# The sine products of a Fourier mixer's hidden layer, from the third chunk on, as three products of 12-bit parts

## The chip, the cores and the metric

The kernel runs on one core of a Trainium2 chip. The metric is the time of one execution on the device in microseconds (us); the kernel before took 1809.15 us (median of three runs, 1809.08 to 1809.34). A core has a matrix engine (TensorE, PE in the rows, its weight loads in rows of their own, PEld), a vector engine (DVE), a scalar engine (ACT), a general one (POOL), and a queue that issues transfers (SP). Each works through its own instructions in order and waits on semaphores for the others.

## The reference

```python
def _attn_ref(x):                       # x: (8, 3008, 256) float32
    X = np.fft.fft(x, axis=1)           # along the sequence
    X = np.fft.fft(X, axis=2)           # along the features
    return X.real.astype(np.float32)

def _moe_ref(x, w_in, w_out):           # x: (24064, 256), w_in: (256, 2048), w_out: (2048, 256)
    h = x @ w_in
    g = np.maximum(0.01 * h, h)         # leaky ReLU
    return (g @ w_out).astype(np.float32)
```

The output is `_moe_ref` of the mixed x, reshaped to 24064 rows. All is float32.

## The kernel before

**Mixing.** The transform along the sequence is done by matrix products with cosine and sine tables after several rounds of folding; the one along the features is folded into `w_in`. Rows k and S-k of the mixed x have the form cos + sin and cos - sin. So the core keeps, for one batch at a time, a cosine half `mix_sb[0]` and a sine half `mix_sb[1]` of 128 partitions by 1505 columns (and the Nyquist row `nb_sb`), and the up product of a pair of rows is one product with the cosine half and one with the sine half. `transform` makes the two halves of one batch and parity, `rows_of_x(0, c)` (cosine) first, then `rows_of_x(1, c)`. Its vector work is put in a list, `folds`, from which `some` emits a little at each step.

**Chunks.** After a first stage of 504 columns with an order written out by hand (`HEAD`, `START`) come 23 chunks of 504 or 498 columns, three to a batch (two in the first). A chunk has 16 steps, one for each 128 rows of the hidden layer (index f). In step f, `up` issues the cosine product into `cos_ps` and the sine product into `sin_ps` (two banks of each, used by turns), each 128 by 128 by 504. ACT copies the cosine bank to `cos_sb` and writes the seed of step f+2 (the Nyquist row times a weight) into the bank; DVE makes cos + sin and cos - sin (`hidden`, the line `nc.vector.tensor_tensor(block.row(to, g, self.n), x, y, op=op)`, L1266); ACT applies the leaky ReLU to them one step later (L1529). The down products use a fast scheme for matrix products: 28 sums of hidden blocks (`SUMS`, on POOL and DVE, L1283), 26 times 4 products of 252 columns (`PRODUCTS`, L1304) with weights that SP streams from memory into a ring `wr`, and 34 sums of results (L1350) on DVE.

**Order.** The program is written out in the order of a list of events, sorted by a time in steps: kind 3 is an up product (at `16 t + 1.20 + f`), kind 1 a sum, kind 2 a down product (6.5 for each step), kind 0 the start of a step, where transforms and loads go on. Each engine's instructions stand in the order in which they are emitted; every engine waits at the front of its own list. A POOL sum is in places made to wait for the DVE instruction ahead of it (`wait_for_gate`).

**Names.** `wf` holds the folded `w_in`, its cosine part (index 0) and its sine part (index 1), in one tile that is const; `block_sb` holds 28 slots of hidden blocks and sums, `part_sb` 24 places for results, `wr` 9 weights.

Of the kernel before, what the change touches and what calls it, by code (L numbers as in the profile page):

```python
# [9 lines left out]
F32 = mybir.dt.float32  # L10
I32 = mybir.dt.int32
# [5 lines left out]
P = 128  # L17
# [310 lines left out]
def tile_fnet_leaky_relu(  # L328
# [21 lines left out]

    block_sb = const.tile([P, SLOTS * SS], F32, name="block")
# [18 lines left out]
    def ring(tag):  # L370
# [5 lines left out]
    assert weights_at - 4 * P >= lay_out(block_sb, 0, (("g", 5, 2 * WN), ("win", 4, WN), ("power", 2, WN), ("raw", 1, 2 * WN), ("o", 2, 2 * WN),  # L376
                                               ("e", 2, 2 * WN), ("s", 4, 2 * WN)))
    head_at = {
        "part": [part_sb, lay_out(part_sb, 0, (("cos", 3, WN), ("out", 2, 2 * WN), ("we", 1, WN), ("nyq", 1, UW[0]))), PARTS * NMAX],
        "cos": [cos_sb.rearrange("p a n -> p (a n)"), 0, 4 * NMAX],  # L380
    }
# [8 lines left out]
    rings["ev"] = [0, [ev_sb, in_head(KC)]]  # L390
    rings["e0"] = [0, [e0_sb, in_head(384)]]
# [100 lines left out]
    class Rows:  # L492
# [3 lines left out]
        def __init__(self, src, scratch, part, c):  # L496
            self.src, self.scratch, self.part, self.c = src[0:ROWS], scratch, part, c
            self.places = PLACES[c] if part else range(16)
# [36 lines left out]
    def rows_of_x(part, c):  # L535

        src = x3[:, 1 - c, :, part * P : (part + 1) * P]
        return Rows(src, [x3[:, 2 * c].rearrange("p c (i d) -> p (c i) d", i=2)], part, c)
# [46 lines left out]
    wf = const.tile([P, 2, F], F32, name="wf")  # L585
# [3 lines left out]
    wt = block_sb[:, weights_at:].rearrange("p (i g n) -> p i g n", g=4, n=P)  # L589
    w_dram = dram.tile([8 + len(W_SUMS), P, 4 * P], F32, name="w_dram")  # L590
    feat_sb = block_sb[:, weights_at - 4 * P : weights_at].rearrange("p (a n) -> p a n", a=2)
    nyx = in_parts(4 * NT * B, 2, 2, NT, B)[0:LOADED]
    nyz = in_parts(16 * B, 16, B)[0:LOADED]
# [120 lines left out]
    def fold_w_in(f0, n, made, tag="up", pieces=1, queue=nc.sync, sums=None):  # L714
# [13 lines left out]
        for odd, at in places:  # L728
            w = m if odd else n
            for i in (1, 0):  # L730
                rows = slice(half, P) if i != odd else slice(0, half)
                nc.scalar.copy(wf[rows, i, f0 + at : f0 + at + w], banks[odd, at][rows, 0:w])
                if i == 1 and odd == 0:
                    spread_wn(f0, n, queue)

    def spread_wn(f0, n, queue):

        for q in range(f0 // P, (f0 + n) // P):
            queue.dma_start(wn[:, q : q + 1], wf[P // 2 : P // 2 + 1, 1, q * P : (q + 1) * P])
# [58 lines left out]

    reach = [w % 4 for w in range(8)]
# [4 lines left out]
    stream = Stream()  # L804
# [219 lines left out]
    def raised(j, f):  # L1024
        b, c, at, n, _ = blocks[j]
        fs = hidden_blocks(j, f)
        pt = raw[j, f] = seeded.get((j, f)) or [up_ps(), up_ps()]
        for blk in range(2):
            for h in range(2):
                nc.tensor.matmul(pt[blk][:, h * n : (h + 1) * n], lhsT=wf[:, blk, fs[h] * P : (fs[h] + 1) * P],  # L1030
                                 rhs=mix_sb[blk][:, at : at + n], start=(h == 0 and (blk == 1 or (j, f) not in seeded)),
                                 stop=(h == 1), skip_group_check=True)
# [186 lines left out]
    class Chunk:  # L1219
# [22 lines left out]
        def touch(self, f, since):  # L1242

            nc.tensor.matmul(cos_ps[self.half(f)][:, since : self.w], lhsT=wf[:, 0, 0:P], rhs=mix_sb[0][:, since : self.w],
                             start=False, stop=True, skip_group_check=True)

# [3 lines left out]
        def up(self, f):  # L1250
            cos, sin = cos_ps[self.half(f)], sin_ps[self.half(f)]
            for i, bank in enumerate((cos, sin)):
                nc.tensor.matmul(bank[:, 0 : self.w], lhsT=wf[:, i, f * P : (f + 1) * P], rhs=mix_sb[i][:, self.lo : self.lo + self.w],  # L1253
                                 start=(i == 1), stop=True, skip_group_check=True)
            k, g = divmod(f, 4)
# [4 lines left out]
            return k, g, copy, sin  # L1260

# [122 lines left out]
    def transform(u, gate):  # L1384
# [4 lines left out]
        first, second = (rows_of_x(part, c) for part in range(2))  # L1389
        for rows in (first, second):  # L1390
            if rows is first:
                load_tabs(0, c)
            rows.fold_even(folds, folds)
            rows.fold_odd(folds, folds)
            if rows is first:
                yield 0, ahead
                made = mix(u, 0, v=folds)
                made[0](even_rows(first, P))
                load_tabs(1, c, (0,))
# [36 lines left out]
    def rest():  # L1436

        count = len(chunk)
        every.extend(Chunk(t) for t in range(count))
        events = []  # L1440
        for t in range(count):
            for f in range(NF):
                events.append((16 * t + UP_FROM + f, 3, t, f))
            for i, s in enumerate(SUMS_AT):
                events.append((16 * t + (s if t < count - 1 else max(s - LAST_SOONER, min(s, 17.05))), 1, t, i))
            for m in range(4 * len(PRODUCTS)):
                events.append((16 * t + (DOWN_FROM + m / PER_STEP if t else FIRST_DOWN + m / FIRST_PER), 2, t, m))
        for r in range(16 * count + 18):
# [50 lines left out]
        for _, kind, t, i in events:  # L1499
            if kind == 0:  # L1500
                start_work(16 * t + i)
                now[0] = START_SHARES.get(i, 0.0) if 16 * t + i < 17 else SHARES[0] if 16 * t + i < 32 else SHARES[1]
# [17 lines left out]
            else:  # L1520
# [11 lines left out]
                behind[:] = [None]  # L1532
                waiting[:] = [part.hidden(*made)]
# [245 lines left out]
```

## Time and profile before

| what | value |
|---|---|
| median of 3 runs | 1809.15 us |
| profiled execution: span from first to last instruction | 1807.9 us |
| median less span (what lies around the span) | 1.25 us |
| PE / DVE / ACT / POOL busy | 100% / 85% / 58% / 57% |
| transfers | 245.88 MB, 136 GB/s over the span |
| granted TensorE clock | 1.000 |

The profile gives no time of the profiled execution other than its span; the median of the runs lies 1.25 us above it. Rows of the timeline read: start in us, length in us, engine, line, operation, what it writes and reads, shape, how many instructions in a row, and in brackets how long the engine had been idle and for whom. A float32 product shows as two MATMUL instructions (x2), each with a weight load. Ends of matmuls are modelled, so the distance from one start to the next, not the length, tells what a product takes.

### The profile page before, as it was taken

Reading aid. Unit: us, or ns where it says so; the run is one execution under the profiler, and the core shown is the slowest. Engines: PE = TensorE matmul, PEld = TensorE weight load, DVE = VectorE, ACT = ScalarE, POOL = GpSimd, SP = SyncE. Lnnn points to the kernel's source line nnn. Section 1 sums busy time; section 2 is a strip of 40 time slices with the busy share of each in tenths; the row PEclk is TensorE's granted clock in tenths of the full one; section 3 lists DMA queues with packets and bytes.
Section 4 is the critical chain, followed back from the end, with each engine's and each line's share of the span. In section 5 each row is a group of like instructions: output and inputs, shape, how many; then the busy total and the mean of one; then the engine's idle time right before and its main releaser. Section 6 shows DMA issues by size and latency. Waiting matters only on the chain.

```text
span 1807.9 us, 22509 instructions
## 1 busy us (share of the span) xinstructions
PE 1801.6 (100%) x7232; PEld 1336.7 (74%) x7232; DVE 1535.2 (85%) x2614; ACT 1042.9 (58%) x1785; POOL 1034.3 (57%) x443
## 2 busy tenths in 40 slices
PE   9999999999999999999999999999999999999999
PEld 7867777777777777777777777777777777777778
DVE  8899888788798987999869988789887897876868
ACT  4687556665556655665556655566555665555540
POOL 2236666766565665755656656556566565566730
PEclk9999999999999999999999999999999999999999
DMA  7365345433363333624435234443333533323324
GB/s 253 104 216 177 95 136 171 149 118 103 117 199 115 122 117 116 223 79 137 135 128 182 90 119 133 150 160 114 128 132 125 173 124 115 122 90 109 121 90 153
DMA packets 144115, 245.88 MB, mean 136 GB/s; under 512 B 17392, under 2 KB 53872, under 8 KB 144000
## 3 DMA queue, kind: packets, MB, share of 16 engines
q1 hardware_dynamic: 143856, 244.46, 41.5%
q8 instruction: 58, 0.95, 0.2%
q14 instruction: 57, 0.47, 0.1%
q10 hardware_dynamic: 144, 0.00, 0.0%
HBM read 212.86 MB, written 31.54 MB: 135 GB/s over the span
## 4 chain that ended last, share of the span: by engine, by line
PE 97%; DVE 1%; ACT 1%; DMA 0%; issue 0%; DVEq 0%
PE sum_psc L1304 21%; PE sum_psa L1304 17%; PE sum_psb L1304 17%; PE sin_psb L1253 9%; PE cos_psb L1253 9%; PE cos_psa L1253 8%; PE sin_psa L1253 8%; PE dft_ps L838 3%; PE sum_psa L1075 1%; PE sum_psc L1075 1%; PE sum_psb L1075 1%; PE dft_ps L1075 1%; PE cos_psa L1030 0%; PE sin_psa L1030 0%; DMA block<-in_w_in_dram 0%; PE sin_psb L1030 0%
## 5 line engine op out<-in xcount | busy, mean ns | idle before, releaser
L1283 POOL TENSOR_TENSOR block<-block 128x1008 f32<-128x1008 f32 (+1 forms) x396 | 995.5, 2525 | 620.2 <-DVE xt L1096 164.1
L1304 PE MATMUL sum_psc<-block,wr 128*128 128x252 f32 (+1 forms) x1832 | 426.0, 375 | 0.8 <-DMA wr<-w_dram 0.8
L1283 DVE TENSOR_TENSOR block<-block 128x1008 f32<-128x1008 f32 (+1 forms) x248 | 417.2, 1687 | 1.5 <-POOL block L1283 1.4
L1304 PEld LDWEIGHTS sum_psc<-block,wr 128*128 128x128 f32 x1832 | 347.8, 190 | 94.7 <-issue 60.4
L1529 ACT ACTIVATE block<-block 128x504 f32<-128x504 f32 (+3 forms) x510 | 393.2, 798 | 4.5 <-DVE block L1266 4.4
L1266 DVE TENSOR_TENSOR block<-cos,sin_psa 128x504 f32<-128x504 f32 (+1 forms) x356 | 224.3, 671 | 150.1 <-PE sin_psa L1253 149.5
L1304 PE MATMUL sum_psb<-block,wr 128*128 128x252 f32 (+1 forms) x1472 | 347.4, 376 | 0.0
L1304 PE MATMUL sum_psa<-block,wr 128*128 128x252 f32 (+1 forms) x1480 | 344.6, 376 | 0.0
L1304 PEld LDWEIGHTS sum_psb<-block,wr 128*128 128x128 f32 x1472 | 277.5, 190 | 85.2 <-issue 56.2
L1304 PEld LDWEIGHTS sum_psa<-block,wr 128*128 128x128 f32 x1480 | 280.5, 190 | 68.2 <-issue 41.0
L1266 DVE TENSOR_TENSOR block<-cos,sin_psb 128x504 f32<-128x504 f32 (+1 forms) x380 | 239.3, 671 | 93.5 <-PE sin_psb L1253 91.9
L1259 ACT COPY cos<-cos_psb 128x504 f32<-128x504 f32 (+1 forms) x190 | 109.5, 576 | 243.5 <-PE cos_psb L1253 243.5
L1259 ACT COPY cos<-cos_psa 128x504 f32<-128x504 f32 (+1 forms) x178 | 102.7, 577 | 244.4 <-PE cos_psa L1253 244.4
L1253 PE MATMUL sin_psb<-mixs,wf 128*128 128x504 f32 (+1 forms) x380 | 191.2, 585 | 0.6 <-DVE block L1266 0.6
L1253 PE MATMUL cos_psb<-mixc,wf 128*128 128x504 f32 (+1 forms) x380 | 191.0, 585 | 0.0
L1350 DVE TENSOR_TENSOR part<-part 128x252 f32<-128x252 f32 (+1 forms) x342 | 183.1, 573 | 1.3
L1253 PE MATMUL cos_psa<-mixc,wf 128*128 128x504 f32 (+1 forms) x356 | 178.9, 584 | 0.0
L1253 PE MATMUL sin_psa<-mixs,wf 128*128 128x504 f32 (+1 forms) x356 | 178.9, 584 | 0.0
L1253 PEld LDWEIGHTS sin_psb<-mixs,wf 128*128 128x128 f32 x380 | 72.1, 190 | 88.9 <-issue 72.9
L1248 ACT ACTIVATE cos_psb<-nb,small 128x504 f32<-128x504 f32 (+1 forms) x190 | 129.8, 683 | 6.2
L1253 PEld LDWEIGHTS sin_psa<-mixs,wf 128*128 128x128 f32 x356 | 67.7, 190 | 82.0 <-issue 67.3
L1248 ACT ACTIVATE cos_psa<-nb,small 128x504 f32<-128x504 f32 (+1 forms) x178 | 121.6, 683 | 5.8
(213 smaller groups left out, 1329.6 us busy)
## 6 DMA issues: line engine op xcount, KB each, us to landing
wr<-w_dram SPq DMA_DIRECT2D x575, 256.0 KB, 3.5
xt<-in_x_dram SPq DMA_DIRECT2D x28, 1024.0 KB, 7.1
out_dram<-part SPq DMA_DIRECT2D x120, 126.0 KB, 1.8
out_dram<-part SPq DMA_DIRECT2D x64, 124.5 KB, 2.0
tabe<-in_seq_tab_dram SPq DMA_DIRECT2D x29, 190.0 KB, 4.0
w_dram<-block SPq DMA_DIRECT2D x18, 256.0 KB, 7.1
block<-in_w_in_dram SPq DMA_DIRECT2D x8, 512.0 KB, 4.4
block<-in_w_out_dram SPq DMA_DIRECT2D x8, 512.0 KB, 5.1
```

The source lines that it names most:

```text
L838: nc.tensor.matmul(o, lhsT=still, rhs=moving, start=(i == 0), stop=(i == 3), skip_group_check=True)
L1075: nc.tensor.matmul(sums[j][d][:, r * n : (r + 1) * n], lhsT=wo[:, fs[h] // 4, fs[h] % 4, d], rhs=a[r][h], start=(f == 0 and r == 0 and h = ...
L1248: nc.scalar.activation(cos_ps[self.half(f)][:, 0 : self.w], nb_sb[:, self.lo : self.lo + self.w], ACT.Copy, scale=wn[:, f : f + 1])
L1253: nc.tensor.matmul(bank[:, 0 : self.w], lhsT=wf[:, i, f * P : (f + 1) * P], rhs=mix_sb[i][:, self.lo : self.lo + self.w], start=(i == 1), ...
L1259: nc.scalar.copy(copy, cos[:, 0 : self.w])
L1266: nc.vector.tensor_tensor(block.row(to, g, self.n), x, y, op=op)
L1283: ins = (engine or nc.gpsimd).tensor_tensor(self.value(16 + i), xa, ya, op=ALU.add if sign > 0 else ALU.subtract)
L1304: nc.tensor.matmul(to, lhsT=stream.weight(self.t, q, g), rhs=self.value(v)[:, g], start=(first and at == 0), stop=(last and g == 3), skip_ ...
L1350: ins = nc.vector.tensor_tensor(part_of[self.copy[v]][:, 0:n], xa, ya, op=ALU.add if sign > 0 else ALU.subtract)
L1529: nc.scalar.activation(to, to, ACT.Lrelu)
```

## The change

From chunk 2 on (21 of the 23 chunks) the sine product of a step is made of three products in the type float32r. Moving and stationary operand are cut into a high part of 12 bits and a low part: high = x times (1 - 2^-13), rounded on writing; for the weights low = (w - high) times 2^12 and both = low - high; for the moving operand low = x - high and both = (1 + 2^-12) high - x. Two products of the parts (index 0 and 1) go into the sine bank, ACT multiplies the bank by 1 + 2^-12 in place, and the third (index 2) is added 0.2 steps later, by an event of a new kind 5, which then issues `hidden` as well. The cosine product is as before.

The parts of the weights are made once, in steps 18 to 25 (during chunk 1), by `parted_weights` on ACT and POOL in turn, stored to memory, and loaded again for each step into four places that the sine part of `wf` leaves free. The parts of the moving operand are made once for each chunk by `parts` on ACT, DVE and POOL, 2.7 steps ahead of the chunk (kind 4). As that reads the sine half before the chunk begins, `transform` now makes the sine half first. To make room, `SLOTS` goes from 28 to 27, `PARTS` from 24 to 18 and `RING` from 9 to 8; some tiles of the first stage move into the new tiles.

```diff
+SLOTS, RS, SS, PARTS = 27, 252, 1008, 18        (was 28, ..., 24)
+RING, RING_AHEAD = 8, 6                         (was 9, 6)
+PARTED_FROM = 2
+UPPER, SHIFT = 1.0 - 2.0**-13, 2.0**12
+PARTS_AT, PARTED_WEIGHTS_AT, UP_END = -2.7, 18, 0.2
...
+    def parted_weights(f):
...
+        nc.scalar.activation(high, src, ACT.Copy, scale=UPPER)
+        wait_for_gate(nc.gpsimd.tensor_tensor(both, src, high, op=ALU.subtract))
+        nc.scalar.activation(low, both, ACT.Copy, scale=SHIFT)
+        nc.gpsimd.tensor_tensor(both, low, high, op=ALU.subtract)
+        nc.sync.dma_start(parted_dram[f : f + 2].rearrange("f p n -> p f n"), here.bitcast(F32).rearrange("p f i n -> p f (i n)"))
...
+    class Parted:
...
+        def load(self, i):
+            n = F // WN
+            if i >= self.count:
+                return
+            if i < n:
+                self.places.append(late.tile([P, 3 * P], F32R, name=f"parted{i}", tag=f"wf{i}"))
+            nc.sync.dma_start(self.places[i % n].bitcast(F32), parted_dram[i % NF])
...
+        def parts(self):
+            m = mixed[self.t % 2].rearrange("p (i n) -> p i n", i=3)
+            high, low, both = (m[:, i, 0 : self.w] for i in range(3))
+            src = mix_sb[1][:, self.lo : self.lo + self.w]
+            nc.scalar.activation(high, src, ACT.Copy, scale=UPPER)
+            nc.vector.scalar_tensor_tensor(both, in0=high, scalar=1.0 + 1.0 / SHIFT, in1=src, op0=ALU.mult, op1=ALU.subtract)
+            nc.gpsimd.tensor_tensor(low, src, high, op=ALU.subtract)
+        def product_of_parts(self, bank, at, i, start=False):
+            m = mixed[self.t % 2].rearrange("p (i n) -> p i n", i=3)
+            nc.tensor.matmul(bank[:, 0 : self.w], lhsT=parted.weight(at, i), rhs=m[:, i, 0 : self.w],
+                             start=start, stop=True, skip_group_check=True)
...
         def up(self, f):
             cos, sin = cos_ps[self.half(f)], sin_ps[self.half(f)]
-            for i, bank in enumerate((cos, sin)):
+            in_parts = self.t >= PARTED_FROM
+            if in_parts:
+                at = NF * (self.t - PARTED_FROM) + f
+                self.product_of_parts(sin, at, 0, start=True)
+                self.product_of_parts(sin, at, 1)
+                nc.scalar.activation(sin[:, 0 : self.w], sin[:, 0 : self.w], ACT.Copy, scale=1.0 + 1.0 / SHIFT)
+            for i, bank in enumerate((cos, sin)[: 2 - in_parts]):
...
+        def up_end(self, f):
+            at = NF * (self.t - PARTED_FROM) + f
+            self.product_of_parts(sin_ps[self.half(f)], at, 2)
+            parted.load(at + F // WN)
...
-        first, second = (rows_of_x(part, c) for part in range(2))
+        first, second = (rows_of_x(1 - i, c, i == 1) for i in range(2))
```

In the two order listings of each place below, `mixed` is the tile of the moving operand's parts, `parted` a place of the weights' parts, and numbers in names tell tiles apart. On PE, in the middle of a chunk, before:

```order
L1253 MATMUL cos_psa<-mixc,wf 128x504
L1253 MATMUL sin_psa<-mixs,wf 128x504
L1304 MATMUL sum_psa<-block,wr 128x252 x6
L1253 MATMUL cos_psb<-mixc,wf 128x504
L1253 MATMUL sin_psb<-mixs,wf 128x504
L1304 MATMUL sum_psb<-block,wr 128x252 x7
```

and in a like step of the changed kernel, on PE (L1315 is the product of parts, L1330 the cosine product, L1388 a down product):

```order
L1315 MATMUL sin_psb<-mixed_966,parted_1155 128x504 x2
L1330 MATMUL cos_psb<-mixc,wf_cos 128x504
L1388 MATMUL sum_psc<-block,wr 128x252
L1315 MATMUL sin_psb<-mixed_966,parted_1155 128x504
L1388 MATMUL sum_psa<-block,wr 128x252 x6
```

The sine products now stand ahead of the cosine product but for the third, which stands behind exactly one down product. On ACT, at step 12 of the chunk that starts at 956 us in the profile, before (copy of the cosine bank, seed, copy of rows of x, leaky ReLU):

```order
L1321 COPY part<-sum_psb 128x252
L1259 COPY cos<-cos_psa 128x504
L1248 ACTIVATE cos_psa<-nb,small 128x504
L1113 COPY dft_ps<-xt 128x512
L1529 ACTIVATE block<-block 128x4x252
L1259 COPY cos<-cos_psb 128x504
```

and now, on ACT at the same place (L1328 scales the bank, L1309 makes the high part of the next chunk's moving operand):

```order
L1405 COPY part<-sum_psb 128x252
L1328 ACTIVATE sin_psa<-sin_psa 128x504
L1338 COPY cos<-cos_psa 128x504
L1319 ACTIVATE cos_psa<-nb,small 128x504
L1168 COPY dft_ps<-xt 128x512
L1622 ACTIVATE block<-block 128x2x252 x2
L1309 ACTIVATE mixed_966<-mixs 128x498
L1328 ACTIVATE sin_psb<-sin_psb 128x504
```

The scaling stands first in the step, the high part last, behind the leaky ReLU. On DVE at the same step, before:

```order
L1094 TENSOR_TENSOR xt<-xt,dft_ps 128x512
L1350 TENSOR_TENSOR part<-part 128x252
L1096 TENSOR_TENSOR xt<-xt 128x512
L1266 TENSOR_TENSOR block<-cos,sin_psa 128x2x252 x2
L1350 TENSOR_TENSOR part<-sum_psb,part 128x252
```

and now, on DVE (L1310 makes the part called both from the high part; L1350 is now `hidden`, L1434 a sum of results):

```order
L1149 TENSOR_TENSOR xt<-xt,dft_ps 128x512
L1434 TENSOR_TENSOR part<-part 128x252
L1151 TENSOR_TENSOR xt<-xt 128x512
L1310 SCALAR_TENSOR_TENSOR mixed_966<-mixed_966,mixs 128x498
L1350 TENSOR_TENSOR block<-cos,sin_psa 128x2x252 x2
L1434 TENSOR_TENSOR part<-sum_psb,part 128x252
```

L1310 stands ahead of that step's `hidden`, and reads what ACT's L1309 writes behind the leaky ReLU of the same step.

More of the change, by code (lines that the diff above doesn't have):

```diff
@@ L10 @@
 F32 = mybir.dt.float32
+F32R = mybir.dt.float32r
 I32 = mybir.dt.int32
@@ L492, in tile_fnet_leaky_relu, with __init__ @@
     class Rows:
-        def __init__(self, src, scratch, part, c):
+        def __init__(self, src, scratch, part, c, second=False):
             self.src, self.scratch, self.part, self.c = src[0:ROWS], scratch, part, c
-            self.places = PLACES[c] if part else range(16)
+            self.places = PLACES[c] if second else range(16)
         def z(self, i, n=None):
@@ L582, in odd_rows_even, with wf @@
             return po
-    wf = const.tile([P, 2, F], F32, name="wf")
+    wf_cos = const.tile([P, F], F32, name="wf_cos")
+    wf_sin = [late.tile([P, WN], F32, name=f"wf_sin{i}", tag=f"wf{i}") for i in range(F // WN)]
+    def wf(i, at, n):
+        if i == 0:
+            return wf_cos[:, at : at + n]
+        return wf_sin[at // WN][:, at % WN : at % WN + n]
     wn = small_sb[:, 0:NF]
@@ L797, in used, with __init__, weight @@
             self.load_to(self.of[t, q] + 1 + RING_AHEAD)
+    mixed = []
+    def parted_weights(f):
+        if not mixed:
+            mixed.extend(late.tile([P, 6 * NMAX], F32R, name=f"mixed{i}", tag=f"mixed{i}") for i in range(2))
+        here = mixed[f // 2 % 2][:, 0 : 6 * P].rearrange("p (f i n) -> p f i n", f=2, i=3)
+        src = wf(1, f * P, 2 * P).rearrange("p (f n) -> p f n", f=2)
+        high, low, both = (here[:, :, i] for i in range(3))
+        nc.scalar.activation(high, src, ACT.Copy, scale=UPPER)
[4 more added lines that the diff above has]
+    class Parted:
+        def __init__(self):
+            self.places, self.count = [], NF * (len(chunk) - PARTED_FROM)
+        def load(self, i):
[5 more added lines that the diff above has]
+            nc.sync.dma_start(self.places[i % n].bitcast(F32), parted_dram[i % NF])
+        def weight(self, i, part):
+            return self.places[i % (F // WN)][:, part * P : (part + 1) * P]
     reach = [w % 4 for w in range(8)]
@@ L803, in tile_fnet_leaky_relu @@
     by_reach = sorted(range(8, len(reach)), key=lambda w: reach[w])
-    stream = Stream()
+    stream, parted = Stream(), None
     def even_rows(rows, m):
@@ L1519, in rest @@
                         some(pool)
-            else:
+            elif kind == 4:
+                every[t].parts()
+            elif kind == 3:
                 if i == 0:
@@ L1532, in rest @@
                 behind[:] = [None]
+                waiting.clear()
+            else:
+                part = every[t]
+                if t >= PARTED_FROM:
+                    part.up_end(i)
                 waiting[:] = [part.hidden(*made)]
```

56 lines of the change are left out of this document (35 added, 21 removed).

## The prediction

> **What bounds the kernel now.** I read the page's busy shares and its chain first, to learn which engine sets the end.
>
> ```profile
> PE 1801.6 (100%) x7232; PEld 1336.7 (74%) x7232; DVE 1535.2 (85%) x2614; ACT 1042.9 (58%) x1785; POOL 1034.3 (57%) x443
> PE 97%; DVE 1%; ACT 1%; DMA 0%; issue 0%; DVEq 0%
> ```
>
> PE is never idle and is 97% of the chain, so every PE microsecond taken away shortens the end, as long as nothing else makes PE wait. What the change takes away I read from the timeline of one step:
>
> ```profile
> 899.83 1.01 PE L1253 MATMUL cos_psa<-mixc,wf 128*128 128x504 f32 x2
> ...
> 900.68 1.01 PE L1253 MATMUL sin_psa<-mixs,wf 128*128 128x504 f32 x2
> 900.68 0.19 PEld L1253 LDWEIGHTS sin_psa<-mixs,wf 128*128 128x128 f32 x1 [0.23 <-issue]
> 900.88 0.58 ACT L1259 COPY cos<-cos_psa 128x504 f32<-128x504 f32 x1 [1.76 <-PE cos_psa L1253]
> ...
> 901.52 2.68 PE L1304 MATMUL sum_psc<-block,wr 128*128 128x249 f32 x12
> 901.52 2.29 PEld L1304 LDWEIGHTS sum_psc<-block,wr 128*128 128x128 f32 x11 [0.23 <-issue]
> ...
> 904.04 1.01 PE L1253 MATMUL cos_psb<-mixc,wf 128*128 128x504 f32 x2
> ```
>
> Start to start a sine product takes 901.52 - 900.68 = 0.84 us (0.845 over several steps), in two instructions of 0.42. The 12 instructions of 249 columns take 904.04 - 901.52 = 2.52, 0.21 each, with 11 weight loads in 2.29 beside them; a load by itself shows 0.19. A step is 2 x 0.845 + 6 (or 7) x 0.42 = 4.22 (or 4.64). ACT sees a product 900.88 - 900.68 = 0.20 after the next one starts.
>
> The next engines are read from the windows of three chunks of one batch (columns: PE, PEld, DVE, ACT, POOL busy) and one of chunk 1:
>
> ```profile
> core 0: us, PE busy (x) PEld busy (x) DVE busy (x) ACT busy (x) POOL busy (x), PEclk, DMA share, GB/s
> 150.00:222.00 72.00, 72.00 (x295) 53.27 (x294) 65.64 (x110) 43.00 (x73) 45.38 (x18) 1.00 0.37 115
> 956.00:1028.00 72.00, 72.00 (x275) 52.12 (x274) 66.21 (x101) 45.89 (x78) 42.84 (x18) 1.00 0.44 140
> 1028.00:1102.00 74.00, 74.00 (x304) 55.14 (x303) 63.90 (x111) 42.94 (x75) 45.75 (x20) 1.00 0.37 119
> 1102.00:1176.00 74.00, 74.00 (x304) 55.14 (x303) 58.85 (x111) 41.86 (x77) 46.21 (x19) 1.00 0.43 142
> ```
>
> DVE has 72 - 66.2 = 5.8 us left in the first chunk of a batch, 10.1 and 15.2 in the others; ACT and POOL have 26 and more. The waits tell who is ahead of whom:
>
> ```profile
> ACT cos L1259 <- PE cos_psa L1253: 244.4, 167, 2.4
> ACT cos L1259 <- PE cos_psb L1253: 243.5, 181, 2.0
> DVE block L1266 <- PE sin_psa L1253: 149.5, 93, 4.0
> DVE block L1266 <- PE sin_psb L1253: 91.9, 64, 3.8
> ```
>
> ACT waits for PE in 348 of 368 steps, 1.4 us each. DVE waits for the sine product in only 157; in the others it comes late, and PE does not mind.
>
> **The PE term.** In 21 chunks x 16 = 336 steps a product of 0.845 gives way to three of float32r, whose price no row shows. Cutting both operands at 12 bits leaves one of the four part-products that a full 24-bit product consists of, so I price one at a quarter of 0.845, 0.211. The upper end is 0.42, one of the two instructions that the float32 product shows; the quarter is the lower end, since one part-product of the four is the least that is left. By the quarter a step gains 0.845 - 0.634 = 0.211 (0.208 at 498 columns): 224 x 0.211 + 112 x 0.208 = **70.6 us**. The loads of the like stream above are hidden beside instructions of 0.21, so I add none.
>
> Against this speaks a rule of the Trainium skill (TensorE: Matmul & The Clock Gate, Part 3, "The mechanism"): a weight load overlaps running matmuls only if it goes to other rows of the array. By that rule each of the three would pay its load too. The 12 products above, on all 128 rows, run at 0.21 with their loads inside, so the trace disagrees for float32; for float32r no run here shows it.
>
> **The wait for the scaling.** The third product waits for ACT. Counted from the start of the first: two products to 0.42, seen by ACT at 0.62; the scaling costs between the copy's 0.58 and the seed's 0.68, done by 1.30; the third is due after the cosine product and one down product, 0.42 + 0.845 + 0.42 = 1.69. That leaves 0.39 if ACT is free. ACT's step at 1010 us:
>
> ```profile
> 1010.01 0.58 ACT L1259 COPY cos<-cos_psa 128x504 f32<-128x504 f32 x1 [0.90 <-PE cos_psa L1253]
> 1010.62 0.69 ACT L1248 ACTIVATE cos_psa<-nb,small 128x504 f32<-128x504 f32 x1
> 1011.24 0.57 ACT L1113 COPY dft_ps<-xt 128x512 f32<-128x512 f32 x1
> 1011.75 1.04 ACT L1529 ACTIVATE block<-block 128x1008 f32<-128x1008 f32 x1
> ...
> 1029.03 1.55 ACT L1121 ACTIVATE dft_ps<-xt,small 95x128 f32<-95x128 f32 x4
> ```
>
> Its copy will start at 0.42 + 0.845 + 0.2 = 1.47, its leaky ReLU end 2.8 later at 4.3, and the next scaling is due at 4.01 + 0.62 = 4.63: it fits. Where four L1121 stand instead of the one copy, ACT is 1.55 - 0.57 = 1.0 longer, 0.7 late, 0.3 beyond the slack. The order has two or so of these in a batch: 7 x 0.5 = **3.5 us** (ends 0 and 7).
>
> **DVE and the high part.** L1310 on DVE waits for ACT's L1309, at 4.3 to 4.9, and costs 0.69 (L673 below), so that step's `hidden` starts at 5.6. Its third product is out at 1.69 + 0.21 + 0.2 = 2.1: 3.5 us late, once in each chunk, in a step where DVE has little idle:
>
> ```profile
> 1010.95 1.27 DVE L1266 TENSOR_TENSOR block<-cos,sin_psa 128x504 f32<-128x504 f32 x2 [0.46 <-PE sin_psa L1253]
> ...
> 1019.83 1.27 DVE L1266 TENSOR_TENSOR block<-cos,sin_psa 128x504 f32<-128x504 f32 x2 [0.43 <-PE sin_psa L1253]
> ...
> 1028.11 3.63 DVE L1350 TENSOR_TENSOR part<-part 128x252 f32<-128x252 f32 x4
> 1031.66 1.24 DVE L1266 TENSOR_TENSOR block<-cos,sin_psa 128x498 f32<-128x498 f32 x2
> ```
>
> The last one's sine product on PE, and three groups (count, then busy us and mean ns, then idle before):
>
> ```profile
> 1027.61 1.00 PE L1253 MATMUL sin_psa<-mixs,wf 128*128 128x498 f32 x2
> ```
>
> ```profile
> L673 DVE SCALAR_TENSOR_TENSOR block<-block 128x512 int32<-128x512 int32 x16 | 11.1, 694 | 0.0
> L1283 POOL TENSOR_TENSOR block<-block 128x1008 f32<-128x1008 f32 (+1 forms) x396 | 995.5, 2525 | 620.2 <-DVE xt L1096 164.1
> L757 POOL TENSOR_TENSOR block<-wr 128x512 f32<-128x512 f32 x6 | 7.6, 1276 | 30.4 <-DVE xt L568 16.4 <-DVE wr L677 12.1 <-DVE xt L1096 1.8
> ```
>
> DVE is on time at 1010.95, idles 0.46 + 0.43 = 0.9 on the way, and is 1031.66 - (1027.61 + 1.00) = 3.05 late four steps on, where four sums beside a busy POOL take it 3.63. Now it starts 3.5 late, catches up by the 0.9, and PE runs 0.2 faster a step: 3.5 + 3.05 - 0.9 + 0.8 = 6.5 late. How much is free? Queued behind a late `hidden` of step f-1 is ACT's leaky ReLU, behind that the scaling of step f+1, and PE waits for that. The scaling must start 0.9 into step f+1, the leaky ReLU (1.1) at -0.2, `hidden` (1.26) at -1.5; its product is out 8.4 - 2.1 = 6.3 before that step, so 4.8 us of lateness is free, and the loss is 6.5 - 4.8 = 1.7 where the first chunk of a batch ends. The other two have the idle to recover; I give them 0.6 together. 7 x 2.3 = **16 us**. Ends: 0, as lateness of 3 cost nothing so far, and 7 a batch, 49, if ACT's copies of x, which wait for DVE as well, take two off the free 4.8 and the other chunks lose as much as the first.
>
> **Making the weights' parts.** In steps 18 to 25 ACT and POOL alternate, two operations each in a step. POOL's are half of L757's 1.28, 16 x 0.64 = 10 us, inside 72 - 45.4 = 26.6 idle in the window at 150; but ACT waits for POOL's, which may stand behind a sum of 2.5 us, and with it the seeds. Ends 0 and 12 (a gain is excluded, PE being full); I take **4 us**, nearer the free end since ACT idles 1.4 a step there.
>
> **What costs nothing.** POOL's low part: 21 x 1.28 = 27 us, inside its 43% of idle. ACT's 336 scalings, 220 us, inside its 42%, leave it at about 73%. Fewer evenly spaced slots split some leaky ReLUs in two (1.13 for 1.04). The transfers:
>
> ```profile
> wr<-w_dram SPq DMA_DIRECT2D x575, 256.0 KB, 3.5
> out_dram<-part SPq DMA_DIRECT2D x120, 126.0 KB, 1.8
> ```
>
> 336 loads of 192 KB add 66 MB to 246. SP issues each behind the third product, four steps (16 us) ahead of use, against some 3.5 to land; if SP stands at a store that waits for a late DVE, those 16 us hide it. The ring of 8 still asks six weights ahead (10 us). With 18 places a place comes back two steps (8 us) after its store, which lands in 2. The swapped halves of `transform` move work of one size.
>
> **Sum**: 1807.9 - 70.6 + 3.5 + 16 + 4 = 1760.8, and with the 1.25 around the span, by which the median lies above this execution, **1762 us**.
>
> **Rivals.** (a) *No loss on DVE and ACT*: PE hides everything. For it: lateness of 3 us costs nothing now. Against: DVE's 5.8 us shrink to 5.8 - 3.4 - 0.7 = 1.7. Time 1739 to 1747. (b) *DVE becomes the bound in every chunk*: for it the 3.5 us of lateness, against it the idle of two chunks in three. With 49 in place of 16: 1795. (c) *The other side*: a float32r product streams no faster than one instruction of float32, 0.42. For it: the trace shows no faster one; against: the 12 bits. Place L1315; 3 x 0.42 - 0.845 = 0.415 more a step, 139 in all: 1948. It decides from 0.258 each, where (0.845 - 23.5 / 336) / 3 lies. (d) *The loads show*: 3 x (0.21 + 0.19) - 0.845 = 0.355 a step, 119: 1928. This is the skill's rule, against which the rows above speak. (e) *The change does not do what it says*: PE waits for ACT in every step and gives back the 0.21. It needs the scaling to come 0.6 later than worked out: about 1808.
>
> **Chances.** Forecast (1748 to 1778) 0.43; (a) 0.21; (b) 0.22, some of it up to 1805; (c) 0.06; (d) 0.03; (e) 0.05. Range 1740 to 1797, which leaves out (c), (d), (e) and the tail of (b), together under 0.2. A change of 0.2%, 3.6 us, is about what can be told from none. Faster 0.87, same 0.04, slower 0.09.
>
> **What would show it.** Starts of L1315 0.21 apart; steps of 4.01 and 4.43; PE's waits for L1328 a few us in all and bunched where four L1176 stand; `hidden` 3 to 6 us late behind each L1310; DVE busy above 90%. I am wrong if L1315 is 0.26 or more apart, if most third products wait, or if PE waits for POOL's sums.

## The result: 1.2% slower, and the profile after

The changed kernel takes 1831.6 us (median of four runs, 1827.8 to 1833.3) against 1809.12 before (1809.04 to 1809.34) on the same chip: a ratio of 1.0121, with a 95% interval of 1.0107 to 1.0135. Forecast were 1762, with a range of 1740 to 1797. The profiled execution took 1830.16, with a span of 1828.0, 20.1 above the span before.

The page's busy times and the shares of its chain, after:

```profile
PE 1769.7 (97%) x7568; PEld 1395.1 (76%) x7568; DVE 1561.5 (85%) x2635; ACT 1251.1 (68%) x2230; POOL 1112.9 (61%) x480
PE 63%; DVE 19%; issue 7%; ACT 7%; POOL 4%; DMA 0%; DVEq 0%; POOLq 0%; ACTq 0%
```

PE's busy time fell by 32 us, but PE is no longer the chain: 97% of it became 63%, and DVE, ACT and POOL now hold 30%. PE idles. The timeline of PE in a step that nothing disturbs shows what the three products cost (start, length, engine, line, operation):

```profile
899.85 0.58 PE L1388 MATMUL sum_psa<-block,wr 128*128 128x249 f32 x2
900.08 0.80 PE L1315 MATMUL sin_psb<-mixed,parted 128*128 128x504 f32 x2
900.72 1.00 PE L1330 MATMUL cos_psb<-mixc,wf_cos 128*128 128x504 f32 x2
901.57 0.58 PE L1388 MATMUL sum_psa<-block,wr 128*128 128x249 f32 x2
901.80 0.57 PE L1315 MATMUL sin_psb<-mixed,parted 128*128 128x504 f32 x1
902.21 2.68 PE L1388 MATMUL sum_psa<-block,wr 128*128 128x249 f32 x12
```

From 899.85 to 900.72 stand a down product (2 x 0.21) and two float32r products: (0.87 - 0.42) / 2 = 0.225 each. From 901.57 to 902.21 a down product and one: 0.22. (The recorded start of a float32r product behind a float32 one is too early: 901.80 lies inside the down product, which lasts from 901.57 to 901.99.) From the starts of all cosine products, undisturbed steps are 0.157 us shorter than before (2.5 a chunk), which makes (0.845 - 0.157) / 3 = 0.229 for each.

I laid the starts of the cosine products of both traces side by side, step by step. After less before, in us:

| chunks | difference | reading |
|---|---|---|
| 0 | 0.0 | nothing changed there |
| 1 (weights' parts are made) | +11.7 | 7.2 of it in one step |
| 2 to 20 | +13.8 | 19 x 2.5 = 47.5 gained, 61.3 lost: 3.2 in each chunk |
| 21 and 22 (no transform beside them) | -4.8 | the whole gain, no loss |

The loss comes in the first five steps of a chunk. Counted from 0, chunks 2, 5, 8 and so on are the first of a batch (504, 504 and 498 columns). From chunk 5 on, the second chunks lose mostly at steps 2 and 4, the third ones (7, 10, 13 and so on) at steps 0 and 1 (+1.2 and +1.35), and the first ones (5, 8, 11 and so on) at step 2 (+2.9, but +5.9 in chunk 11 and +4.7 in chunk 14). The waits of the changed kernel (engine and line, what it waited for: us in all, times, longest) name who was late:

```profile
DVE mixed L1310 <- ACT mixed L1309: 52.7, 20, 3.6
PE sin_psa L1315 <- ACT sin_psa L1328: 29.7, 19, 2.9
PE sin_psb L1315 <- ACT sin_psb L1328: 7.7, 9, 1.2
ACT dft_ps L1168 <- DVE xt L1149: 36.6, 28, 2.6
ACT dft_ps L1176 <- DVE xt L1151: 26.7, 8, 3.6
ACT dft_ps L1176 <- DVE xt L1173: 13.1, 5, 2.7
ACT block L1622 <- DVE block L1350: 16.2, 19, 2.5
ACT mixed L833 <- POOL mixed L832: 20.0, 8, 5.6
```

Before, ACT's waits for DVE were these:

```profile
ACT dft_ps L1121 <- DVE xt L1096: 13.4, 8, 2.3
ACT block L1529 <- DVE block L1266: 4.4, 6, 1.2
```

So a circle of three engines stands there: DVE waits for ACT's high part once in a chunk, ACT waits for DVE in its share of the transform of x (L1168, L1176) and in the leaky ReLU (L1622), and PE's third product waits for ACT's scaling (L1328). Following each of PE's 28 waits for L1328 (19 + 9) back along ACT shows the order: in 27 of them ACT had, just ahead, stood idle for DVE at an L1168 or L1176, for 1.15 to 3.6 us. So ACT was not short of time there; it waited. One such stall in chunk 8, from the timelines of DVE, PE and ACT:

```profile
660.84 0.68 DVE L1310 SCALAR_TENSOR_TENSOR mixed<-mixed,mixs 128x504 fp32r<-128x504 f32 x1 [2.43 <-ACT mixed L1309]
...
681.03 1.26 DVE L1350 TENSOR_TENSOR block<-cos,sin_psa 128x504 f32<-128x504 f32 x2
...
682.54 2.11 DVE L1367 TENSOR_TENSOR block<-block 128x996 f32<-128x996 f32 x1
684.57 1.27 DVE L1151 TENSOR_TENSOR xt<-xt 95x256 f32<-95x256 f32 x4
```

```profile
676.11 0.58 PE L1315 MATMUL sin_psa<-mixed,parted 128*128 128x504 f32 x1
...
682.94 0.80 PE L1315 MATMUL sin_psa<-mixed,parted 128*128 128x504 f32 x2
...
687.79 0.50 PE L1315 MATMUL sin_psa<-mixed,parted 128*128 128x504 f32 x1 [2.79 <-ACT sin_psa L1328]
```

```profile
685.01 0.77 ACT L1176 ACTIVATE dft_ps<-xt,small 95x128 f32<-95x128 f32 x2 [3.57 <-DVE xt L1151]
685.72 1.03 ACT L1622 ACTIVATE block<-block 128x1008 f32<-128x1008 f32 x1
...
687.16 0.58 ACT L1328 ACTIVATE sin_psa<-sin_psa 128x504 f32<-128x504 f32 x1
```

DVE lost 2.43 at L1310, and `hidden` (L1350) starts at 681.03, 4.5 us behind its third product (676.11 + 0.41). ACT, however, is held not by that `hidden`, which ends at 682.2, but by its own L1176 ahead of the leaky ReLU: this waits for DVE's L1151, which stands behind `hidden` and behind a sum of 2.11. ACT idles 3.57, and the scaling, due at 682.94 + 0.62 = 683.56, starts at 687.16. PE stops for 2.79.

Chunk 1 has a stall of another make. From the timelines of POOL, ACT, DVE and PE:

```profile
181.89 4.60 POOL L1367 TENSOR_TENSOR block<-block 128x1008 f32<-128x1008 f32 x2
186.44 0.73 POOL L832 TENSOR_TENSOR mixed<-wf_sin,mixed 128x256 fp32r<-128x256 f32 x1
```

```profile
187.21 0.42 ACT L833 ACTIVATE mixed<-mixed 128x256 fp32r<-128x256 f32 x1 [3.26 <-POOL mixed L832]
```

```profile
188.12 1.26 DVE L1350 TENSOR_TENSOR block<-cos,sin_psa 128x498 f32<-128x498 f32 x2 [5.10 <-ACT cos L1338]
```

```profile
191.49 1.62 PE L893 MATMUL dft_ps<-tabo,xt 95*128 95x95 f32 x8 [4.25 <-DVE xt L1173]
```

POOL's part stands behind two sums, ACT's second operation behind POOL's part, the cosine copy behind that, and then DVE and PE.

A part of the loss is the clock of TensorE. In chunk 11 PE stops for 2.76 us, up to 909.37, and this follows (two rows of PE, and a row of windows with the columns that the prediction shows):

```profile
909.96 3.52 PE L1388 MATMUL sum_psb<-block,wr 128*128 128x249 f32 x8
913.27 1.86 PE L893 MATMUL dft_ps<-tabe,xt 95*128 95x95 f32 x8
909.00:915.50 6.50, 6.13 (x20) 5.33 (x20) 6.50 (x12) 2.71 (x5) 4.03 (x2) 0.50 0.36 107
```

The eight down instructions take (913.27 - 909.96) / 8 = 0.41 each in place of 0.21, at a granted clock of 0.50. The clock is 0.50 in three stretches of this execution, each at the end of a stop of PE or just behind it: 3.41 us in chunk 1 (stop of 4.25), 6.83 in chunk 11 (2.76) and 3.41 in chunk 14 (2.89). At half the clock they cost up to half their length, 1.7, 3.4 and 1.7 us; chunks 11 and 14 are 3.5 and 2.3 us longer than before, the like chunks 5, 8, 17 and 20 only 0.5 to 0.7. So 5.1 of the 61.3 us and 1.7 of the 11.7 are the clock's. Four more stops of 2.8 to 2.9 us were not followed by a lower clock. The four runs of the changed kernel differ in the same way: spans of 1825.6 and 1831.1 us come with mean clocks of 0.997 and 0.994, which is about 5.5 and 11 us lost.

### The profile page after: what moved, and what is told of

It reads as the page before. It is cut to its first block, busy times and chain, and to the rows that moved or that the text cites. A ratio compares the mean times of both kernels' runs of the same rounds, so it can differ in the third digit from the quotient of the medians.

```text
span 1828.0 us, 24121 instructions
## 1 busy us (share of the span) xinstructions
PE 1769.7 (97%) x7568; PEld 1395.1 (76%) x7568; DVE 1561.5 (85%) x2635; ACT 1251.1 (68%) x2230; POOL 1112.9 (61%) x480
## 4 chain that ended last, share of the span: by engine, by line
PE 63%; DVE 19%; issue 7%; ACT 7%; POOL 4%; DMA 0%; DVEq 0%; POOLq 0%; ACTq 0%
PE sum_psc L1388 14%; PE sum_psb L1388 12%; PE sum_psa L1388 11%; DVE block L1367 6%; PE cos_psb L1330 5%; PE cos_psa L1330 5%; DVE block L1350 5%; PE sin_psa L1315 4%; PE sin_psb L1315 4%; DVE part L1434 4%; POOL block L1367 3%; PE dft_ps L893 2%; ACT block L1622 2%; DVE xt L1151 1%; ACT dft_ps L1176 1%
## 5 line engine op out<-in xcount | busy, mean ns | idle before, releaser
L1367 POOL TENSOR_TENSOR block<-block 128x1008 f32<-128x1008 f32 (+1 forms) x396 | 1020.8, 2590 | 545.1 <-DVE xt L1151 149.0
L1388 PE MATMUL sum_psc<-block,wr 128*128 128x252 f32 (+1 forms) x1832 | 442.9, 375 | 0.2 <-DVE block L1367 0.2
L1388 PEld LDWEIGHTS sum_psc<-block,wr 128*128 128x128 f32 x1832 | 346.8, 190 | 96.8 <-issue 60.6
L1622 ACT ACTIVATE block<-block 128x504 f32<-128x504 f32 (+3 forms) x582 | 400.7, 723 | 16.3 <-DVE block L1350 16.2
L1388 PE MATMUL sum_psb<-block,wr 128*128 128x252 f32 (+1 forms) x1472 | 369.1, 379 | 0.9 <-POOL block L1367 0.9
L1388 PE MATMUL sum_psa<-block,wr 128*128 128x252 f32 (+1 forms) x1480 | 358.7, 376 | 5.7 <-DVE part L1434 5.7
L1388 PEld LDWEIGHTS sum_psb<-block,wr 128*128 128x128 f32 x1472 | 279.5, 192 | 89.9 <-issue 60.6
L1388 PEld LDWEIGHTS sum_psa<-block,wr 128*128 128x128 f32 x1480 | 279.2, 190 | 78.2 <-issue 41.2
L1350 DVE TENSOR_TENSOR block<-cos,sin_psa 128x504 f32<-128x504 f32 (+1 forms) x356 | 223.9, 669 | 99.8 <-PE sin_psa L1315 85.2
L1350 DVE TENSOR_TENSOR block<-cos,sin_psb 128x504 f32<-128x504 f32 (+1 forms) x380 | 238.8, 669 | 69.6 <-PE sin_psb L1315 62.6
L1315 PE MATMUL sin_psa<-mixed,parted 128*128 128x504 f32 (+1 forms) x504 | 229.0, 508 | 31.1 <-ACT sin_psa L1328 29.7
L1315 PE MATMUL sin_psb<-mixed,parted 128*128 128x504 f32 (+1 forms) x504 | 230.3, 511 | 8.0 <-ACT sin_psb L1328 7.7
L1434 DVE TENSOR_TENSOR part<-part 128x252 f32<-128x252 f32 (+1 forms) x342 | 203.5, 632 | 1.3
L1330 PE MATMUL cos_psb<-mixc,wf_cos 128*128 128x504 f32 (+1 forms) x380 | 191.0, 584 | 1.4 <-ACT cos_psb L1319 1.4
L1330 PE MATMUL cos_psa<-mixc,wf_cos 128*128 128x504 f32 (+1 forms) x356 | 179.5, 585 | 0.9 <-ACT cos_psa L1319 0.9
L1328 ACT ACTIVATE sin_psa<-sin_psa 128x504 f32<-128x504 f32 (+1 forms) x168 | 96.8, 576 | 109.5 <-PE sin_psa L1315 109.0
L1328 ACT ACTIVATE sin_psb<-sin_psb 128x504 f32<-128x504 f32 (+1 forms) x168 | 96.2, 572 | 77.5 <-PE sin_psb L1315 75.7
L1315 PEld LDWEIGHTS sin_psa<-mixed,parted 128*128 128x128 f32 x504 | 95.1, 190 | 53.5 <-ACT sin_psa L1328 38.7
```

What stands on the lines that cost most here:

```text
L1315: nc.tensor.matmul(bank[:, 0 : self.w], lhsT=parted.weight(at, i), rhs=m[:, i, 0 : self.w], start=start, stop=True, skip_group_check=True)
L1328: nc.scalar.activation(sin[:, 0 : self.w], sin[:, 0 : self.w], ACT.Copy, scale=1.0 + 1.0 / SHIFT)
L1330: nc.tensor.matmul(bank[:, 0 : self.w], lhsT=wf(i, f * P, P), rhs=mix_sb[i][:, self.lo : self.lo + self.w], start=(i == 1), stop=True, ski ...
L1367: ins = (engine or nc.gpsimd).tensor_tensor(self.value(16 + i), xa, ya, op=ALU.add if sign > 0 else ALU.subtract)
L1388: nc.tensor.matmul(to, lhsT=stream.weight(self.t, q, g), rhs=self.value(v)[:, g], start=(first and at == 0), stop=(last and g == 3), skip_ ...
L1434: ins = nc.vector.tensor_tensor(part_of[self.copy[v]][:, 0:n], xa, ya, op=ALU.add if sign > 0 else ALU.subtract)
```

## The experiments

The theories at the start. *Q* (for queue): the step from ACT back to PE inside a step is what costs, because ACT, working in order, hands DVE's lateness on through the scaling. *D*: L1310 and the shorter steps make DVE the bound, and the scaling only shows it. Where an expectation has Q1 and Q2, these are Q with DVE's wait at L1310 as the source of the lateness, and Q with the lateness there anyway. Each kernel below starts from the changed one, and "lost" is what PE loses in chunks 2 to 20 against 2.5 us gained in each, read from the cosine starts as above, in the profiled execution. The clock has a share in "lost": 5 us in the changed kernel, 2 with `both` later, 7 with the weights' parts apart, up to 31 with the third product later, and none in the other kernels (half the length of the stretches at 0.50).

| kernel | median us | ratio to before, 95% | chunk 1 | lost in chunks 2 to 20 |
|---|---|---|---|---|
| changed kernel | 1831.6 | 1.0121 (1.0107 to 1.0135) | +11.7 | 61 |
| rearranged only | 1809.57 | 1.0002 (0.9992 to 1.0011) | | |
| no scaling | 1805.87 | 0.9982 (0.9972 to 0.9991) | +12.6 | 36 |
| no share of x on ACT | 1804.21 | 0.9974 (0.9964 to 0.9984) | +11.8 | 35 |
| `both` later | 1809.67 | 1.0004 (0.9995 to 1.0013) | +12.4 | 40 |
| no scaling and `both` later | 1787.53 | 0.9880 (0.9865 to 0.9894) | +13.1 | 18 |
| weights' parts a step apart | 1820.91 | 1.0069 (1.0054 to 1.0084) | +4.7 | 63 |
| third product later | 1913.22 | 1.0575 (1.0559 to 1.0591) | +12.2 | 136 |
| without low times low | 1767.18 | 0.9768 (0.9753 to 0.9783) | +1.6 | 9 |
| the same, cosine first | 1758.07 | 0.9717 (0.9701 to 0.9733) | +0.9 | 1 |

### Without the scaling

```diff
-                nc.scalar.activation(sin[:, 0 : self.w], sin[:, 0 : self.w], ACT.Copy, scale=1.0 + 1.0 / SHIFT)
```

> The changed kernel without ACT's scaling of the sine bank (the multiplication by 1 + 2^-12 is left out; everything else stands). Theory Q (queue): the 63 us that PE loses in chunks 2 to 20 come from ACT's order: the scaling stands in ACT's list behind an operation that waits for a late DVE, and PE waits for the scaling. Then nearly all of these waits go, only those for DVE itself (about 1 us a batch, 7 to 9 us) and chunk 1's 12 us stay: 1772 to 1785 us. Theory D (DVE has too much to do in the shorter step, whoever waits for it): PE's waits move from the scaling to the release of the sine bank by DVE; little is won: 1815 to 1828 us.

1805.87 us: 25.7 come back, between the two theories. The waits show what is left once ACT no longer stands between DVE and PE:

```profile
DVE mixed L1310 <- ACT mixed L1309: 52.6, 20, 3.5
PE dft_ps L893 <- DVE xt L1173: 12.8, 8, 4.3
PE sin_psa L1315 <- DVE block L1349: 9.9, 14, 1.6
PE sum_psa L1387 <- DVE part L1433: 8.4, 6, 1.5
```

PE now waits for DVE itself: for a sine bank that `hidden` has not yet read, for the rows of x that PE transforms, for a place in a sum. DVE is as late as before the edit, and part of that lateness reaches PE without ACT. Neither theory alone is enough. The loss in chunks 2 to 20 falls from 61 to 36 us; 5 of this difference are the clock's, which here stays at 1.00 in these chunks.

### The part called both later

DVE's L1310 is issued 1.2 steps behind ACT's high part, as an event of its own, so DVE need not wait for it.

```diff
             nc.scalar.activation(high, src, ACT.Copy, scale=UPPER)
-            nc.vector.scalar_tensor_tensor(both, in0=high, scalar=1.0 + 1.0 / SHIFT, in1=src, op0=ALU.mult, op1=ALU.subtract)
             nc.gpsimd.tensor_tensor(low, src, high, op=ALU.subtract)
...
                 events.append((16 * t + PARTS_AT, 4, t, 0))
+                events.append((16 * t + PARTS_AT + 1.2, 4, t, 1))
...
-                every[t].parts()
+                every[t].both_part() if i else every[t].parts()
```

> The changed kernel with DVE's part (both) of the moving operand issued 1.2 steps later than the high and low parts, behind the next step's hidden, so that DVE no longer stands idle for ACT's high part (52.7 us of waiting over 20 chunks in the changed kernel, 2.6 each). Theory Q1: this wait is the main source of DVE's lateness at the start of the next chunk; without it each chunk loses 1 us instead of 3: 1788 to 1800 us. Theory Q2: DVE's lateness there comes from its load and the shorter steps, and the wait is made good before the next chunk starts: 1822 to 1832 us.

1809.67 us: 21.9 come back, again between the ranges. Waits:

```profile
PE sin_psa L1320 <- ACT sin_psa L1333: 22.1, 15, 2.2
ACT dft_ps L1176 <- DVE xt L1151: 22.4, 8, 2.9
```

The wait of 52.7 at L1310 is gone from DVE. What DVE was late already (3.05 us in the rows of before that the prediction shows) and the shorter steps are enough to keep PE waiting for the scaling: 22.1, from 29.7.

### Both edits together

> Both edits together: no scaling of the sine bank (left out), and DVE's part issued 1.2 steps later. One alone took 26 and 22 us off. Theory: these are two causes, DVE's wait makes it late, and the scaling carries the lateness to PE; with both gone PE's losses in chunks 2 to 20 fall from 9 us a batch to 1.3 to 2.6, chunk 1's 12 stay: 1776 to 1786 us. Rival: the two are substitutes for each other, and what is left is DVE's load: 1796 us or more.

1787.53 us, 44 below the changed kernel, 1.5 above the expected range and 8.5 below the rival's. The two causes nearly add up (25.7 + 21.9 = 47.6); in chunks 2 to 20 and without the clock's share the two edits alone bring 20.2 and 17.4, and both together 38.1. Of the 18 us still lost, PE's waits show DVE again:

```profile
PE dft_ps L893 <- DVE xt L1173: 8.9, 8, 4.3
```

### Without ACT's share of the transform of x

The first experiments show that ACT carries the lateness, not which of its operations does: the leaky ReLU, which the prediction had followed, or L1168 and L1176 ahead of it, as the timeline of chunk 8 suggests. Here these two are left out from step 17 on, so the kernel no longer computes the whole transform; one copy fills the bank that DVE still reads.

```diff
-            self.queue.append((0.0, None, lambda: nc.scalar.copy(copy, y)))
+            self.queue.append((0.0, None, lambda: None))
...
-            self.queue.append((0.0, None, lambda: nc.scalar.activation(to, x, f, scale=scale)))
+            self.queue.append((0.0, None, lambda: None if self.copies else nc.scalar.activation(to, x, f, scale=scale)))
...
             folds.copies = True
+            nc.scalar.copy(misc_ps[:, 0:512], wf_cos[:, 0:512])
```

> The kernel after, with ACT's share of the transform of x left out from step 17 on: the copies (L1168) and the four multiplications of a turn (L1176) are not issued, so DVE's operations of the transform read what stands in the bank; everything else, and its order, is as in the kernel after. Theory X (the lateness of DVE reaches PE through these operations, which wait for DVE and stand ahead of ACT's scaling): most of the 63 us that PE loses in chunks 2 to 20 come back, 1775 to 1800 us, and PE's waits for L1328, 38 us now, fall to under 12. Theory R (the leaky ReLU, which waits for a late hidden, carries the lateness by itself): little comes back, 1815 to 1832 us, and PE's waits for L1328 stay above 30. Chunk 1's 11.7 us stay under both.

1804.21 us, 4 above the range of theory X and 11 below that of R. The waits, among them PE's for the scaling:

```profile
ACT block L1622 <- DVE block L1350: 70.8, 64, 3.4
PE dft_ps L893 <- DVE xt L1173: 12.1, 8, 3.5
PE sin_psa L1315 <- DVE block L1350: 8.5, 12, 1.5
PE sin_psb L1315 <- ACT sin_psb L1328: 0.9, 1, 0.9
PE sin_psa L1315 <- ACT sin_psa L1328: 0.3, 2, 0.2
```

PE's waits for the scaling fall from 37.4 us to 1.2, although the leaky ReLU now waits 70.8 us for `hidden` in place of 16.2. So the leaky ReLU alone hands on almost nothing, as the prediction had worked out, and ACT's operations on x hand on nearly all of PE's wait for the scaling; this fits the 27 of 28 waits above. What is left, 35 us, is the same as without the scaling (36), with the same waits of PE for DVE: the two edits cut one path at two places. This run also takes ACT's work for these operations and DVE's waits for them away, so the sizes are not those of the wait alone.

### The third product later

```diff
-PARTS_AT, PARTED_WEIGHTS_AT, UP_END = -2.7, 18, 0.2
+PARTS_AT, PARTED_WEIGHTS_AT, UP_END = -2.7, 18, 0.8
```

> The changed kernel with the third product 0.8 instead of 0.2 steps behind the first two (four or five down products between instead of one), which gives the scaling 2.5 us more before PE waits, and lets hidden come 2.5 us later. Theory: what PE lacks is slack between the scaling and the third product; its waits for the scaling (89 us recorded over matmuls and loads, in the same places) fall by more than half: 1795 to 1812 us. Rival: hidden comes later, so do the leaky ReLU and the next scaling, and the wait is only handed on: 1825 us or more.

1913.22 us, in the rival's range, which has no upper end, and far above its 1825. Waits:

```profile
DVE block L1350 <- ACT block L1622: 107.5, 64, 2.9
ACT block L1622 <- DVE block L1350: 93.4, 54, 5.8
PE sin_psa L1315 <- DVE block L1350: 48.1, 26, 4.0
```

The slack given to the scaling is taken from DVE: `hidden` comes with the third product, 0.6 steps later, and ACT and DVE wait for each other. PE's waits for the scaling do fall, from 37.4 us to 7.9, as the theory said, but now PE waits for DVE to read the sine bank. Its many stops of 2 to 4 us bring the clock's share from 5 us to as much as 31 of the 136 lost.

### Only the rearrangement

```diff
-PARTED_FROM = 2
+PARTED_FROM = 23
...
-                if 0 <= 16 * t + i - PARTED_WEIGHTS_AT < NF // 2:
-                    parted_weights(2 * (16 * t + i - PARTED_WEIGHTS_AT))
```

> All that the change moves, without the parts: sine half first, 27 slots, 18 places for results, a ring of 8, tiles in their new places, but float32 sine products in all chunks and no parts of the weights. Theory: none of this costs anything: 1806 to 1812 us. Rival: the smaller room or the order of the halves makes DVE late by itself and has a share in the loss: 1814 us or more.

1809.57 us, no change. The sine half first, 27 slots, 18 places and a ring of 8 cost nothing that can be measured; the whole difference comes from the parts.

### The weights' parts a step apart

The second operations of ACT and POOL on a pair of weights' parts, and the store, are issued one step behind the first.

```diff
         wait_for_gate(nc.gpsimd.tensor_tensor(both, src, high, op=ALU.subtract))
+        later_weights.append((f, here))
+
+    def parted_weights_end():
...
         nc.scalar.activation(low, both, ACT.Copy, scale=SHIFT)
...
+                parted_weights_end()
                 if 0 <= 16 * t + i - PARTED_WEIGHTS_AT < NF // 2:
```

> The changed kernel with ACT's and POOL's second operations on the weights' parts issued one step later, so that ACT does not wait for POOL within a step. Theory: the 11.7 us that chunk 1 loses come from ACT's waits for POOL (20.0 us over 8 times): chunk 1 loses 0 to 4 us, the whole 1820 to 1825 us. Rival: POOL is overloaded there (16 operations more between sums) and PE waits for its sums and for what follows them anyway: chunk 1 loses 9 us or more, the whole 1828 to 1833 us.

1820.91 us, as expected. ACT's waits of this kind:

```profile
ACT mixed L841 <- POOL mixed L832: 5.4, 5, 1.9
```

They fall from 20.0 us to 5.4, a new wait of 7.2 us (4 times) for the stores of the parts to leave their places comes in, and chunk 1 loses 4.7 in place of 11.7. The other chunks lose what they lost: 63, or 56 without the clock's share, as in the changed kernel (61 and 56).

### Three products with no step through ACT

High times high, high times low and low times high need no scaling between them if the weights' low part is left unscaled, and no part called both. Low times low is left out.

```diff
-                self.product_of_parts(sin, at, 0, start=True)
-                self.product_of_parts(sin, at, 1)
-                nc.scalar.activation(sin[:, 0 : self.w], sin[:, 0 : self.w], ACT.Copy, scale=1.0 + 1.0 / SHIFT)
+                for n, (i, j) in enumerate(((0, 0), (0, 1), (1, 0))):
+                    self.product_of_parts(sin, at, i, j, start=(n == 0))
...
-            self.product_of_parts(sin_ps[self.half(f)], at, 2)
```

> Three one-pass products of another kind: high x high, high x low and low x high, with the low parts unscaled, all three ahead of the cosine product; the product of the two low parts, some 2^-26 of the whole, is left out. Then there is no scaling, no part called both, no late third product, and half the work on the weights' parts. A step without waits takes 0.16 us less than before, as in the changed kernel: 336 x 0.16 = 54 us. Theory Q: nothing on PE's way depends on ACT within the step any more, as before the change; with 0 to 4 us lost in chunk 1 and 0 to 10 at the starts of chunks: 1755 to 1769 us. Theory D: DVE's load in shorter steps costs as much as in the changed kernel: 1800 us or more.

1767.18 us, in the expected range. With the gain on PE intact and neither a step through ACT nor L1310, only 9 us are lost. Three products in a row on PE:

```profile
1000.67 1.03 PE L1312 MATMUL sin_psb<-mixed,parted 128*128 128x504 f32 x3
1001.54 1.01 PE L1326 MATMUL cos_psb<-mixc,wf_cos 128*128 128x504 f32 x2
```

0.87 less the 0.2 by which such a start is recorded early is 0.67, or 0.22 each: the order of the products does not matter for their price.

DVE's longest sum of waits in this kernel is for the copy of the cosine bank, as the sine products come first:

```profile
DVE block L1345 <- ACT cos L1334: 149.3, 116, 3.2
```

The last experiment puts the cosine product ahead of the three.

> The kernel without the low-low product (1767 us) with the cosine product ahead of the three sine products, as before the change. There DVE's hidden waits for ACT's copy of the cosine bank (149 us over 116 steps), since the copy starts only behind all products. Theory: with the copy beside the sine products hidden starts 0.5 us sooner and the rest of DVE's lateness shrinks: 1757 to 1764 us. Rival: DVE's late places lie at the starts of chunks, where it does not wait for the copy at all: 1765 to 1768 us.

1758.07 us, as expected, 2.8% below the kernel before and the best of all. Its waits and its page's busy times:

```profile
ACT dft_ps L1174 <- DVE xt L1149: 29.9, 14, 3.8
```

```profile
PE 1748.8 (100%) x7568; PEld 1396.0 (79%) x7568; DVE 1578.5 (90%) x2614; ACT 1064.3 (61%) x1886; POOL 1107.5 (63%) x472
```

PE is at 100% again, and chunks 3 to 22 are each 2.4 to 2.6 us shorter. ACT still waits for DVE, 29.9 us at this one line, and PE loses almost nothing by it (1 us in chunks 2 to 20): no product of PE waits for ACT within the step.

## Why the prediction was wrong, point by point

| term | forecast | measured |
|---|---|---|
| PE, 336 steps | -70.6 | 19 x -2.5 - 4.8 = -52.3 |
| wait for the scaling, and DVE's lateness | 3.5 + 16 | 61.3 (chunks 2 to 20; 5.1 of it the clock's) |
| weights' parts | 4 | 11.7 (chunk 1; 1.7 of it the clock's) |
| sum, of the span | -47.1 | +20.7 (span: +20.1) |

**The PE term**: right in kind, too large by 18 us. "Cutting both operands at 12 bits leaves one of the four part-products", 0.211, was only the lower end; measured are 0.229. The decision point of rival (c), 0.258, was not reached, and (c) and (d) are refuted. The Trainium skill's rule on weight loads (TensorE: Matmul & The Clock Gate, Part 3, "The mechanism") does not hold here for float32r either. The page's group of these loads:

```profile
L1315 PEld LDWEIGHTS sin_psa<-mixed,parted 128*128 128x128 f32 x504 | 95.1, 190 | 53.5 <-ACT sin_psa L1328 38.7
```

With loads of 0.19 showing, a product would take 0.40; it takes 0.229 with its load.

**DVE and the high part**: "L1310 on DVE waits for ACT's L1309 [...] `hidden` starts [...] 3.5 us late, once in each chunk" was right: 20 waits of 2.6 us on the mean, 3.6 at most, and 0.68 for L1310 itself (in chunk 8's row).

**"so 4.8 us of lateness is free"** is the step that failed. The path followed went from `hidden` to the leaky ReLU to the scaling. On ACT stand L1168 and L1176 ahead of that leaky ReLU; they wait for DVE's work on x, which stands behind `hidden` and a sum. In chunk 8 a lateness of 4.5, inside the 4.8, cost 2.79. The prediction named these copies, but gave them two microseconds and only in its upper end; the run without them, in which 1.2 of 37.4 us are left, shows that they carried nearly all of PE's wait for the scaling. Their rows were in the trace before, 13.4 us of waits of L1121 for DVE: harmless then, as ACT had nothing on which PE depended in the same step.

**"The other two have the idle to recover"** failed with it. All three chunks of a batch lose about 3 us each without the clock's share, those with the most idle too: DVE's idle over a chunk does not help within the five steps in which it is late. (The windows that the prediction calls the first, second and third chunk of a batch, from 956, 1028 and 1102 us, are chunks 12 to 14: the second and third of one batch and the first of the next, by their widths of 504, 498 and 504. Its sum does not depend on this.) The run without scaling adds that DVE gets later than thought: PE writes a sine bank again 8.4 us after the first product into it (steps of 4.01 and 4.43), the third product is out at 2.1, and `hidden` takes 1.26, so where PE waits for `hidden` (9.9 us, 14 times there) it is more than 5.0 late.

**The wait for the scaling**: the slack of 0.39 that was worked out for a free ACT holds; without the operations on x PE waits 1.2 us for the scaling in 336 steps. The 3.5 us of the sum were for the four L1176 that make ACT's step longer; that run leaves these out as well, so it does not test the 3.5.

**Weights' parts**: "ACT waits for POOL's, which may stand behind a sum of 2.5 us" was what happened, but behind two sums (4.60), and with ACT went the copy, DVE and PE. I leaned on ACT's 1.4 us idle a step; the longest wait was 5.6. The upper end, 12, was right in size, with 1.7 us of the clock in it.

**What costs nothing** was right: rooms and order of halves by the run with the rearrangement alone (1809.57), which has none of the new loads; the loads by the waits of the changed kernel, in which no product of parts waits for a transfer. The page gives the new loads 2.8 us to land:

```profile
parted<-parted_dram SPq DMA_DIRECT2D x336, 192.0 KB, 2.8
```

**The rivals**: (b), "DVE becomes the bound in every chunk", was nearest in kind with 1795, but only half of it: DVE's lateness alone costs 36 us, the way through ACT 20 more, and the clock 5. (e) named ACT's wait in every step; it comes in bunches. No rival had the circle of DVE, ACT and PE, and neither sum nor rivals had a lower clock behind PE's stops.

**Open**: the 18 us left with no scaling and `both` later against 9 without low times low. The two differ above all in L1310 and in the place of the third product, which I did not separate. Also open is why three of the seven stops of 2.7 us or more were followed by half the clock and four were not.

## What to carry to other kernels

When a change puts an engine with in-order work between two instructions of the bound engine, go through all that stands ahead of the new instruction in its queue, operation by operation, and ask for each what it waits for: idle share says nothing on this, as ACT idled 32% and still held PE. A lateness that is harmless in the profile before is harmless only for the dependences that existed then. Rather than widen the slack (the third product later cost 82 us more, up to 27 of them by the clock), take the engine out of the loop: products that can be accumulated with nothing between them kept the whole gain.

## What the runs showed of the hardware

A float32r product of 128 by 128 by 504 takes 0.229 us from start to start, 0.018 above a quarter of the float32 product's 0.845, three in a row or apart alike; what the 0.018 are was not tried. The granted TensorE clock fell to 0.50 behind some of PE's stops, for 3.41 or 6.83 us at a time, and a down instruction then took 0.41 us in place of 0.21. In the changed kernel this followed stops of 4.25, 2.76 and 2.89 us, but not four others of 2.8 to 2.9. Over the span the mean clock was 1.000 in the kernels in which PE had no gaps (before, and the two without low times low), 0.996 in the changed kernel, and 0.982 in the one with the third product later, where sixteen such stretches cost PE up to 34 us.
